# Another pace for the transform steps of the second and the third batch

## The chip, the cores and the metric

One core of one Trainium2 chip runs the kernel. The metric is device time in microseconds (us). TensorE is called PE here, VectorE DVE, ScalarE ACT, GpSimd POOL and SyncE SP; PE and PEld are the products and the weight loads of TensorE.

## The reference

Eight batches of 3136 tokens with 256 channels go through a filter in the frequency domain, and then through a mixing layer and a two-layer perceptron with a residual:

```python
    X = np.fft.rfft(x, axis=1)
    F = (filt_r + 1j * filt_i)[None, :, :]
    Y = X * F
    y = np.fft.irfft(Y, n=x.shape[1], axis=1)
...
    X = np.fft.fft(x, axis=1)
    X = np.fft.fft(X, axis=2)
    mixed = np.real(X).astype(np.float32)
    u = x + mixed
    mu = np.mean(u, axis=-1, keepdims=True)
    var = np.mean((u - mu) ** 2, axis=-1, keepdims=True)
    un = (u - mu) / np.sqrt(var + 1e-06)
    ch = np.maximum(un @ w_ch1, 0.0) @ w_ch2
    return (u + ch).astype(np.float32)
```

The second part's x is the first part's y; `w_ch1` is 256 x 1024, `w_ch2` 1024 x 256.

## The kernel before

All products run in float16 on numbers split into a high and a low part; a product of two split numbers is three matmuls. 3136 is 112 x 28, so each transform is done in two stages of matrix products with a store to DRAM and a load between them.

The work of a batch b has two halves, written as generators whose `yield`s cut them into steps.

*Forth*, `there(b)`, 63 steps (`STEPS`): `forward1` loads the batch in seven parts `x_b_0..6` (L410), takes the greatest absolute value of each on DVE (`absmax`, L289) for a scale, and forms 14 products of the first stage, `s1` (L431), between a split of x into float16 (L425 on ACT, L426 on DVE) and a split of the result (`ast`, L433 and L434) that is stored to `d1` (L435). `forward2` loads it turned (`at`, L456), forms the second stage in seven chunks (`s2`, L481 and L482), multiplies by the filter on DVE and POOL (`yt`, `t`, L491 to L505), folds even and odd parts into a ring of frequencies (`eo`), turns the product with DMA transposes (`z`), and forms the first stage of the inverse (`i1`, L551 to L553), which is stored to `d2` as `bt` (L560).

*Home*, `back(b)`, 17 steps (`BACK`): `inverse2` loads `b2` (L594), forms the second stage of the inverse, `y_b_c` (L617), and stores the scaled result `ys` (L626) to `dy` (L600).

The perceptron takes the 8 x 3136 tokens in 49 groups of 512 (256 slots of two tokens). For a group g: `fetch(g)` loads the filtered tokens y (L687). `prepare(g)` forms the transform over channels, `mix_g` (L700), adds it to y on DVE (L710), normalises (statistics at L769 and L770, scale `sb` at L781 to L785, `un` on ACT at L792), splits the result into `u16` (L795 on ACT, L797 on POOL, on DVE in groups 0 and 1), and turns it by two DMA transposes into `ut` (L804). Then come eight first products `h_g_f` (L828, six matmuls of 512 columns each), each followed by a relu on ACT (L837) and the low part on DVE (L838), and eight second products into `acc_g` (L857, twelve matmuls of 256 columns each), which follow two first products behind (`LAG`). A last add (L866) and a store (L869) end the group.

The order of the work is set in the main loop (L1038 to L1055), which counts first products with q, eight to a group: one first product, a piece of the preparation of the group after next, one second product, one home step if it is due, and then as many forth steps as `advance` is told by a pace (L1051). `bring` (L983) asks for what a fetch needs if the pace hasn't yet brought it. `advance(n)` issues forth steps until n have been issued in all; step n belongs to batch n // 63. It stops ahead of a batch until the home steps of the batch before the last are out, and ahead of a fold while the ring still holds frequencies that a mix needs. Beyond this, a scheduler that works with estimated times settles the order of the instructions on each engine, and semaphores and buffers what waits for what: four PSUM banks are shared in turn by `s1`, `s2`, `i1`, `y` and `mix`, two hold `h`, two `acc`; seven large buffers are shared by x, `at` and `z`. SP issues all loads, stores and transposes in one queue.

Of the kernel before, what the change touches and what calls it, by code (L numbers as in the profile page):

```python
# [38 lines left out]
STEPS = FIRST + PAUSE + 7 * 5  # L39
WAIT = 2  # L40
BACK = 1 + WAIT + 14
EARLY = 0.6
RISE = 28
SOON = 994
LOADED = 300
LOAD_AT = (31, 31, 35, 35, 50, 50, 54, 54)
LOAD_AFTER = (("at", 2), ("at", 2), ("at", 3), ("at", 3), ("bt", 3), ("bt", 3), ("bt", 4), ("bt", 4))
# [142 lines left out]
def program(tc, a, NB):  # L190
    nc = tc.nc
    with ExitStack() as ctx:
        _program(ctx, tc, nc, a, NB)


def _program(ctx, tc, nc, a, NB):
# [482 lines left out]
    def fetch(g):  # L679
        y = ys_of[g] = mp.tile([128, 2, 2, 256], F32, tag="y", name=f"y_{g}", bufs=4)  # L680
        for t, (g0, g1) in enumerate(groups[g]):
            q = g0
            while q < g1:
                b = q // NS
                e = min(g1, (b + 1) * NS)
                with after(("un", 0)) if g == 2 else after(("out", g - 4)):
                    marks["y", g] = nc.sync.dma_start(  # L687
                        y[q - g0 : e - g0, t], dys[b][:, q - b * NS : e - b * NS].rearrange("k s c -> s k c")
                    ).ins
                q = e  # L690
# [123 lines left out]
    def first_product(g, f):  # L814
        y, ut = ready[g]
        m = groups[g][0][1] - groups[g][0][0]
        nt = 2 * sum(g1 - g0 for g0, g1 in groups[g])
        utv = ut[:, : len(groups[g])].rearrange("p t (k d l) q -> p t k d l q", k=2, d=2)
        p = ps_h.tile([128, 512], F32, tag="psh", name=f"h_{g}_{f}")
        even = nt == 2 * m * len(groups[g])  # L820
        runs = [(slice(0, len(groups[g])), 0, nt, m)] if even else [
            (slice(t, t + 1), 256 * t, 2 * (g1 - g0), g1 - g0) for t, (g0, g1) in enumerate(groups[g])
        ]
        for ts, c0, n, m in runs:
            i = 0
            for d in range(2):
                for hw, hx in ((0, 0), (0, 1), (1, 0)):
                    marks["pe"] = nc.tensor.matmul(  # L828
                        p[:, c0 : c0 + n].rearrange("p (t k q) -> p t k q", k=2, q=m),
                        w1s[:, d, hw, 128 * f : 128 * f + 128],  # L830
                        utv[:, ts, :, d, hx, :m],
                        start=i == 0,
                        stop=i == 5,
                    ).ins
                    i += 1
        h = mp.tile([128, 2, 512], F16, tag="h", name=f"h16_{g}_{f}", bufs=4)
        nc.scalar.activation(h[:, 0, :nt], p[:, :nt], AF.Relu)  # L837
        marks["h"] = nc.vector.scalar_tensor_tensor(  # L838
            h[:, 1, :nt], p[:, :nt], 0.0, h[:, 0, :nt], op0=ALU.max, op1=ALU.subtract
        ).ins  # L840
        hs[g, f] = h

    def second_product(g, f):
        tiles = groups[g]
        y = ready[g][0]
        h = hs.pop((g, f))
        if f == 0:
            accs[g] = [
                ps_o.tile([128, 2, 256], F32, tag="pso", name=f"acc_{g}_{t}") for t in range(len(tiles))
            ]  # L850
        c0 = 0
        for t, (g0, g1) in enumerate(tiles):
            m = g1 - g0
            acc = accs[g][t]
            for k in range(2):
                for i, (hh, hw) in enumerate(((0, 0), (0, 1), (1, 0))):
                    nc.tensor.matmul(  # L857
                        acc[:m, k],
                        h[:, hh, c0 : c0 + m],
                        w2s[:, f, hw],  # L860
                        start=f == 0 and k == 0 and i == 0,
                        stop=f == 7 and k == 1 and i == 2,
                    )
                c0 += m
            if f == 7:
                nc.vector.scalar_tensor_tensor(  # L866
                    y[:m, t], acc[:m], beta[:m], y[:m, t], op0=ALU.mult, op1=ALU.add
                )
                marks["sp"] = marks["out", g] = nc.sync.dma_start(a["out"][:, g0:g1].rearrange("k s c -> s k c"), y[:m, t]).ins  # L869
# [86 lines left out]
    def advance(n):  # L956

        while done[0] < min(n, NB * STEPS):
            b, s = divmod(done[0], STEPS)
            if s == 0 and come[0] < BACK * (b - 1) + 1:  # L960
                return
            if s in folds and b * NS + folds[s] - RING > mixed[0]:
                return
            next(forth)
            done[0] += 1

    def give(n):

        while come[0] < min(n, NB * BACK) and done[0] >= STEPS * (come[0] // BACK + 1) - 1:
            next(home)  # L970
            come[0] += 1
# [3 lines left out]
    def need(slot):  # L975

        return BACK * (slot // NS) + 1 + WAIT + 2 + 2 * (slot % NS // 224)

    def soon(slot):

        return max(need(slot), BACK * ((slot + LOADED) // NS) + 1 + WAIT)

    def bring(slot):  # L983
        advance(STEPS * (slot // NS + 1) - 1)
        give(need(slot))
        assert come[0] >= need(slot)
# [48 lines left out]
    for _ in range(AHEAD):  # L1035
        next(work, None)
    per = NS // 32
    for q in range(8 * ng + LAG):  # L1038
        g, f = divmod(q, 8)
        if g < ng:  # L1040
            first_product(g, f)
        if f == 8 - AHEAD:
            for _ in work:
                pass
            if g + 2 < ng:
                work = prepare(g + 2)
        next(work, None)
        if q >= LAG:
            second_product(*divmod(q - LAG, 8))
        give(min(come[0] + 1, soon(32 * q + SOON)))  # L1050
        advance(int(STEPS * (1 + min((q + 1) / RISE, (q + 1) / per + EARLY))))  # L1051
        for ahead in [2] * (q == 0) + [g + 3] * (f == 6):
            if ahead < ng:
                bring(groups[ahead][-1][1] - 1)
                fetch(ahead)  # L1055
# [59 lines left out]
```

## Time and profile before

| | |
|---|---|
| median of 3 runs | 1497.44 us (1496.48 to 1500.48) |
| the profiled execution's own time | 1497.62 us |
| its span, first to last instruction | 1495.8 us |
| PE busy | 1426.8 us, 95% of the span |
| DVE busy | 1101.7 us, 74% |
| ACT busy | 768.5 us, 51% |
| POOL busy | 532.1 us, 36% |
| mean granted clock of PE | 0.984 of full speed |

Busy time is the time in which an engine executes at least one instruction. The granted clock is the share of its full clock that PE was allowed. The page also cuts the span into 40 slices, of 37.4 us each; a digit is the busy share of a slice in tenths:

```profile
PE   8897999959999999999999999999999999999998
DVE  6888878588778786787668787798778886555552
POOL 3840077008600583008600384107710474010110
PEclk9997999989999999999999999999999999999999
```

The ninth digit of PE is the slice from 299 to 337 us. POOL's digits rise and fall with the second stages of the batches, which come in its work as blocks: slices 6 and 7 hold those of the second batch, 10 and 11 those of the third.

### The profile page before, as it was taken

How to read it: one execution, taken by the hardware profiler on the slowest of the kernel's cores; microseconds unless marked ns; L12 is line 12 of the kernel's file. 1: busy time of each engine (PE TensorE's matmuls, PEld its weight loads, DVE VectorE, ACT ScalarE, POOL GpSimd, SP SyncE). 2: the span in 40 equal slices, each digit the busy share in tenths (PEclk: the TensorE clock that was granted, in tenths of full speed). 3: DMA queues.
4: the chain of work that ended last, by engine and by line, in shares of the span. 5: the costliest groups of instructions: out<-in, count | busy, mean ns of one | idle time of the engine just before them, and what ended most of it. 6: DMA issues, size and time to landing. Idle time of an engine off the chain costs nothing.

```text
span 1495.8 us, 30721 instructions
## 1 busy us (share of the span) xinstructions
PE 1426.8 (95%) x11553; PEld 944.6 (63%) x11553; DVE 1101.7 (74%) x2398; ACT 768.5 (51%) x1418; POOL 532.1 (36%) x674
## 2 busy tenths in 40 slices
PE   8897999959999999999999999999999999999998
PEld 3644576536766667666766677667666667666666
DVE  6888878588778786787668787798778886555552
ACT  4764745365536555465545555465545655344331
POOL 3840077008600583008600384107710474010110
PEclk9997999989999999999999999999999999999999
DMA  8866597769884996769874896859775995554320
GB/s 323 282 189 200 144 199 182 228 180 240 191 248 133 213 235 169 219 171 222 193 227 122 215 246 150 255 156 243 181 212 162 226 242 138 161 124 107 87 57 29
DMA packets 445076, 280.46 MB, mean 187 GB/s; under 512 B 218688, under 2 KB 410496, under 8 KB 444928
## 3 DMA queue, kind: packets, MB, share of 16 engines
q1 hardware_dynamic: 444928, 278.51, 71.3%
q8 instruction: 90, 1.47, 0.4%
q14 instruction: 58, 0.48, 0.1%
HBM read 124.78 MB, written 102.79 MB: 152 GB/s over the span
## 4 chain that ended last, share of the span: by engine, by line
PE 64%; DMA 12%; DVE 11%; issue 4%; SPq 3%; ACT 2%; POOL 2%; DVEq 0%; ACTq 0%; POOLq 0%
PE h L828 25%; PE acc L857 24%; DMA x<-x 3%; DMA at<-d 3%; PE y L617 3%; PE s L431 3%; DVE y L710 2%; PE mix L700 2%; DMA d<-ast 2%; DMA z<-y 1%; PE i L551 1%; DVE h L838 1%; DVE mx L289 1%; PE s L481 1%; PE i L553 1%
## 5 line engine op out<-in xcount | busy, mean ns | idle before, releaser
L857 PE MATMUL acc<-w2s,h 128*128 128x256 f16 x4704 | 595.5, 273 | 2.3 <-DVE y L866 1.2
L828 PE MATMUL h<-ut,w1s 128*128 128x512 f16 x2352 | 582.3, 380 | 7.7 <-DVE h L838 6.7
L857 PEld LDWEIGHTS <-h 128*128 128x128 f16 x4704 | 454.5, 98 | 142.0 <-issue 9.0
L837 ACT ACTIVATE h<-h 128x512 f16<-128x512 f32 x392 | 232.8, 595 | 378.6 <-PE h L828 371.1
L838 DVE SCALAR_TENSOR_TENSOR h<-h,h 128x512 f16<-128x512 f32 x392 | 266.7, 682 | 196.1 <-ACT h L837 195.1
L797 POOL TENSOR_TENSOR u<-un,u 128x512 f16<-128x512 f32 x94 | 107.5, 1158 | 767.1 <-ACT u L795 679.4
L828 PEld LDWEIGHTS <-w1s 128*128 128x128 f16 x2352 | 221.3, 98 | 213.4 <-issue 26.2
L710 DVE SCALAR_TENSOR_TENSOR y<-mix,alpha,y 128x508 f32<-128x508 f32 (+1 forms) x368 | 156.1, 474 | 8.4 <-PE mix L700 7.2
L792 ACT ACTIVATE un<-y,sb 128x256 f32<-128x256 f32 x196 | 101.9, 590 | 41.5 <-DVE sb L785 37.1
L505 POOL TENSOR_TENSOR y<-yt,y 128x448 f16<-128x448 f32 x105 | 107.9, 1032 | 21.4 <-ACT y L504 21.2
L626 ACT ACTIVATE ys<-y,alpha 128x512 f32<-128x512 f32 x112 | 76.2, 685 | 72.5 <-PE y L617 71.2
L559 DVE TENSOR_TENSOR bt<-i,bt 112x512 f16<-112x512 f32 x112 | 75.7, 682 | 44.9 <-ACT bt L558 43.3
L499 POOL TENSOR_TENSOR yt<-yt,t 128x224 f32<-128x224 f32 x112 | 76.5, 683 | 72.6 <-DVE t L495 47.5
L491 DVE SCALAR_TENSOR_TENSOR yt<-s,pF,ft 128x448 f32<-128x448 f32 x112 | 75.4, 675 | 29.4 <-PE s L482 23.3
L431 PE MATMUL s<-x,s 112*112 112x512 f16 x294 | 88.2, 390 | 7.6 <-DVE y L710 2.7
L289 DVE TENSOR_REDUCE mx<-x 112x1 f32<-112x1024 f32 x56 | 67.5, 1212 | 33.3 <-DMA x<-x 33.0
L558 ACT CAST bt<-i 112x512 f16<-112x512 f32 x112 | 64.4, 583 | 51.6 <-PE i L553 47.7
L866 DVE SCALAR_TENSOR_TENSOR y<-acc,beta,y 128x512 f32<-128x512 f32 x98 | 71.2, 742 | 24.5 <-PE acc L857 24.4
L481 PE MATMUL s<-s,at 112*128 112x56 f16 x896 | 62.5, 190 | 22.9 <-DMA at<-d 22.0
L434 DVE TENSOR_TENSOR ast<-s,ast 112x512 f16<-112x512 f32 x98 | 66.8, 682 | 22.3 <-ACT ast L433 21.9
L504 ACT CAST y<-yt 128x448 f16<-128x448 f32 x112 | 62.8, 564 | 39.2 <-POOL yt L500 38.2
L433 ACT CAST ast<-s 112x512 f16<-112x512 f32 x98 | 57.0, 582 | 47.5 <-PE s L431 40.6
(137 smaller groups left out, 1729.7 us busy)
## 6 DMA issues: line engine op xcount, KB each, us to landing
x<-x SPq DMA_DIRECT2D x56, 512.0 KB
at<-d SPq DMA_DIRECT2D x56, 512.0 KB
b<-d SPq DMA_DIRECT2D x56, 512.0 KB
d<-ast SPq DMA_DIRECT2D x112, 224.0 KB
d<-bt SPq DMA_DIRECT2D x112, 224.0 KB
out<-y SPq DMA_DIRECT2D x98, 256.0 KB
y<-dy SPq DMA_DIRECT2D x92, 256.0 KB
dy<-ys SPq DMA_DIRECT2D x208, 112.0 KB
```

The lines of the kernel that those rows point to most:

```text
L289: nc.vector.tensor_reduce(dst, src, axis=axis, op=ALU.max, apply_absolute_value=True)
L431: nc.tensor.matmul(p, s1[:, hs], x16[:, hx], start=i == 0, stop=i == 2)
L481: nc.tensor.matmul(o, w, s2[:, U, 0].rearrange("p (r k) -> p r k", r=2), start=True, stop=False)
L499: nc.gpsimd.tensor_tensor(yh[:, 0], yh[:, 0], t2v[:, 1], op=ALU.subtract)
L505: last = half(b, hf == 1).tensor_tensor(ylo, ytv, yhi, op=ALU.subtract)
L710: nc.vector.scalar_tensor_tensor(out, p, al, y, op0=ALU.mult, op1=ALU.add)
L792: nc.scalar.activation(un[:m, k], y[:m, t, k], AF.Identity, bias=sb[:m, i, 1:2], scale=sb[:m, i, 3:4])
L797: marks["u16", g] = low.tensor_tensor(u16[:m, :, :, 1], unv, u16[:m, :, :, 0], op=ALU.subtract).ins
L828: marks["pe"] = nc.tensor.matmul(p[:, c0 : c0 + n].rearrange("p (t k q) -> p t k q", k=2, q=m), w1s[:, d, hw, 128 * f : 128 * f + 128], ut ...
L837: nc.scalar.activation(h[:, 0, :nt], p[:, :nt], AF.Relu)
L838: marks["h"] = nc.vector.scalar_tensor_tensor(h[:, 1, :nt], p[:, :nt], 0.0, h[:, 0, :nt], op0=ALU.max, op1=ALU.subtract).ins
L857: nc.tensor.matmul(acc[:m, k], h[:, hh, c0 : c0 + m], w2s[:, f, hw], start=f == 0 and k == 0 and i == 0, stop=f == 7 and k == 1 and i == 2,)
```

## The change

The pace of the forth steps is a new function of the count of first products, with three lines of which the lowest holds.

```diff
+HEAD = 8
+HOLD = 36
+CATCH = 32
...
     per = NS // 32
+
+    def pace(q):
+
+        second = STEPS + HEAD + (STEPS - HEAD) * q / RISE
+        third = 2 * STEPS + max(0, q - HOLD) * STEPS / CATCH
+        return min(second, third, STEPS * (1 + EARLY + q / per))
+
     for q in range(8 * ng + LAG):
...
-        advance(int(STEPS * (1 + min((q + 1) / RISE, (q + 1) / per + EARLY))))
+        advance(int(pace(q + 1)))
```

With `STEPS` 63, `RISE` 28, `EARLY` 0.6 and `per` 49: before, 65 steps were out after the first product 0 (two of the second batch), 63/28 = 2.25 more after each product, and all 126 of two batches at product 28; the third batch went on at that pace until the other line, 63/49 = 1.29 steps a product, came below it at product 39. Now 72 are out after product 0 (nine of the second batch), 55/28 = 1.96 more after each, and 126 at product 28 as before; then none until product 36, and from there 63/32 = 1.97 a product until the line of 1.29 is met at product 67. At product 39 the third batch is 19 steps behind where it was. From there on, the fourth batch and all later ones go as before. Line numbers of the changed kernel are higher by 3, from the loop on by 10.

On the engines the order differs from the first group's products to about group 16. Three places of it:

On DVE, in the first group's hidden tiles (`h16_0_f`, the low part of hidden tile f of group 0; `mx_1<-x_1_q`, absmax of part q of the second batch; `y_1`, adds of group 1). Before:

```order
L838 SCALAR_TENSOR_TENSOR h16_0_0_1682<-h_0_0_1675,h16_0_0_1682 128x512
L770 BN_AGGR mv_1_1651<-st_1_1652 128x2
L769 BN_STATS st_1_1652<-y_1_1622 128x6 x2
L838 SCALAR_TENSOR_TENSOR h16_0_1_1712<-h_0_1_1705,h16_0_1_1712 128x512
L289 TENSOR_REDUCE mx_1_1699<-x_1_0_1692 112x1
L770 BN_AGGR mv_1_1651<-st_1_1652 128x2 x2
L838 SCALAR_TENSOR_TENSOR h16_0_2_1725<-h_0_2_1718,h16_0_2_1725 128x512
L289 TENSOR_REDUCE mx_1_1699<-x_1_1_1693 112x1
L289 TENSOR_REDUCE mx_1_1699<-x_1_2_1694 112x1
```

and now:

```order
L841 SCALAR_TENSOR_TENSOR h16_0_0_1682<-h_0_0_1675,h16_0_0_1682 128x512
L292 TENSOR_REDUCE mx_1_1699<-x_1_0_1692 112x1
L292 TENSOR_REDUCE mx_1_1699<-x_1_1_1693 112x1
L292 TENSOR_REDUCE mx_1_1699<-x_1_2_1694 112x1
L292 TENSOR_REDUCE mx_1_1699<-x_1_3_1695 112x1
L292 TENSOR_REDUCE mx_1_1699<-x_1_4_1696 112x1
L713 SCALAR_TENSOR_TENSOR y_1_1622<-mix_1_1625,alpha_0_373,y_1_1622 128x2x127 x2
L713 SCALAR_TENSOR_TENSOR y_1_1622<-mix_1_1625,alpha_0_373,y_1_1622 128x4
L292 TENSOR_REDUCE mx_1_1699<-x_1_5_1697 112x1
L773 BN_AGGR mv_1_1651<-st_1_1652 128x2 x2
L841 SCALAR_TENSOR_TENSOR h16_0_1_1723<-h_0_1_1716,h16_0_1_1723 128x512
```

Five reductions moved ahead of the second hidden tile and of the last adds of group 1; before, the first of them stood behind that tile, in ones and twos.

On SP, behind the last stores of the second batch's first inverse stage (`b2_1_c`, loads of its home transform; `x_2_q`, loads of the third batch; `ut_5`, transposes of group 5). Before:

```order
L594 DMA b2_1_0_3330<-d2_1_130 128x8x256
L410 DMA x_2_0_3332<-x 128x1024
L410 DMA x_2_1_3333<-x 128x1024
L410 DMA x_2_2_3334<-x 128x1024
L410 DMA x_2_3_3335<-x 128x1024
L410 DMA x_2_4_3336<-x 128x1024
L410 DMA x_2_5_3337<-x 128x1024
L594 DMA b2_1_1_3411<-d2_1_130 128x8x256
L804 DMA_TRANSPOSE ut_5_3352<-u16_5_0_3453 128x8x128
L804 DMA_TRANSPOSE ut_5_3352<-u16_5_1_3495 128x8x128
```

and now the place at which the loads of the third batch stand, behind the fetches of group 6 and among those of group 7:

```order
L597 DMA b2_1_3_3526<-d2_1_130 128x8x256
L690 DMA y_7_3735<-dy_1_3329 128x2x256
L603 DMA dy_1_3329<-ys_1_4_3528 28x4x256 x4
L413 DMA x_2_0_3658<-x 128x1024
L413 DMA x_2_1_3659<-x 128x1024
L413 DMA x_2_2_3660<-x 128x1024
L413 DMA x_2_3_3661<-x 128x1024
L413 DMA x_2_4_3662<-x 128x1024
L690 DMA y_7_3735<-dy_1_3329 128x2x256
L597 DMA b2_1_4_3767<-d2_1_130 128x8x256
L413 DMA x_2_5_3663<-x 128x1024
```

The loads of x moved from ahead of the transposes of group 5 to behind them, by some twenty rows.

On DVE, the preparation of group 6 (`y_6`, its adds; `st_6`, `mv_6`, its statistics; `ast_2`, `x16_2`, splits of the third batch's first stage; `h16_g_f`, low parts). Before:

```order
L838 SCALAR_TENSOR_TENSOR h16_5_7_4374<-h_5_7_4367,h16_5_7_4374 128x512
L434 TENSOR_TENSOR ast_2_2_3598<-s1_2_2_3594,ast_2_2_3598 112x2x256
L426 SCALAR_TENSOR_TENSOR x16_2_5_3706<-x_2_2_3334,sx_2_3530,x16_2_5_3706 112x512
L710 SCALAR_TENSOR_TENSOR y_6_3436<-mix_6_3612,al_6_0_3751,y_6_3436 128x4x127
L710 SCALAR_TENSOR_TENSOR y_6_3436<-mix_6_3612,al_6_0_3751,y_6_3436 128x2x127 x2
L710 SCALAR_TENSOR_TENSOR y_6_3436<-mix_6_3612,al_6_0_3751,y_6_3436 128x4
L710 SCALAR_TENSOR_TENSOR y_6_3436<-mix_6_3612,alpha_1_2225,y_6_3436 128x4x127
L866 SCALAR_TENSOR_TENSOR y_5_3002<-acc_5_0_4043,beta_96,y_5_3002 128x512
L866 SCALAR_TENSOR_TENSOR y_5_3002<-acc_5_1_4044,beta_96,y_5_3002 128x512
L710 SCALAR_TENSOR_TENSOR y_6_3436<-nyq_6_0_3621,alpha_1_2225,keep_6_3749 1x2x127
L769 BN_STATS st_6_3814<-y_6_3436 128x6
L710 SCALAR_TENSOR_TENSOR y_6_3436<-mix_6_3612,alpha_1_2225,y_6_3436 128x2x127 x2
```

and now its end:

```order
L841 SCALAR_TENSOR_TENSOR h16_4_7_3745<-h_4_7_3738,h16_4_7_3745 128x512
L772 BN_STATS st_6_3679<-y_6_3419 128x6 x2
L292 TENSOR_REDUCE mx_2_3665<-x_2_0_3658 112x1
L772 BN_STATS st_6_3679<-y_6_3419 128x6
L292 TENSOR_REDUCE mx_2_3665<-x_2_1_3659 112x1
L773 BN_AGGR mv_6_3678<-st_6_3679 128x2 x2
L292 TENSOR_REDUCE mx_2_3665<-x_2_2_3660 112x1
L841 SCALAR_TENSOR_TENSOR h16_5_0_3787<-h_5_0_3780,h16_5_0_3787 128x512
L773 BN_AGGR mv_6_3678<-st_6_3679 128x2
L292 TENSOR_REDUCE mx_2_3665<-x_2_3_3661 112x1
L292 TENSOR_REDUCE mx_2_3665<-x_2_4_3662 112x1
L841 SCALAR_TENSOR_TENSOR h16_5_1_3828<-h_5_1_3821,h16_5_1_3828 128x512
```

The adds of group 6 moved from behind group 5's last hidden tile, among the first-stage steps of the third batch, to ahead of group 4's last hidden tile, where no such step stands; the reductions of the third batch now stand around group 5's first. On PE, the mix of group 6 goes with them, from product 47 to product 37, the first y product of the second batch from product 37 to 34, and the mix of group 7 stands directly ahead of the first product of group 6.

## The prediction

> **What bounds the kernel now.** I read the head of the page first, then the idle time of the PE stage by stage, then the waits behind it.
>
> The page, its head and one group row:
>
> ```profile
> span 1495.8 us, 30721 instructions
> PE 1426.8 (95%) x11553; PEld 944.6 (63%) x11553; DVE 1101.7 (74%) x2398; ACT 768.5 (51%) x1418; POOL 532.1 (36%) x674
> ...
> L289 DVE TENSOR_REDUCE mx<-x 112x1 f32<-112x1024 f32 x56 | 67.5, 1212 | 33.3 <-DMA x<-x 33.0
> ```
>
> PE is busy for 95% of the span, so a new order of the same work can win only what PE loses: 1495.8 - 1426.8 = 69.0 us of idle time, and what a reduced clock adds to its busy time. The windows show where that lies in the stretch that the change touches. The columns are start and end, length, then busy time and instructions of PE, PEld, DVE, ACT and POOL, the granted clock of PE, DMA share and GB/s:
>
> ```profile
> 130.00:150.00 20.00, 20.00 (x133) 12.60 (x132) 20.00 (x44) 5.72 (x10) 0.00 (x0) 1.00 0.26 69
> 150.00:160.00 10.00, 6.33 (x33) 3.50 (x31) 8.35 (x32) 8.49 (x17) 0.00 (x0) 0.84 0.61 157
> ...
> 180.00:200.00 20.00, 18.83 (x187) 12.63 (x185) 16.74 (x41) 8.49 (x16) 4.26 (x6) 1.00 0.74 182
> 200.00:230.00 30.00, 29.60 (x329) 22.41 (x328) 24.24 (x51) 14.39 (x28) 28.67 (x41) 1.00 0.94 195
> 230.00:260.00 30.00, 27.83 (x241) 20.61 (x238) 27.06 (x54) 17.25 (x36) 23.20 (x30) 1.00 0.75 178
> 260.00:290.00 30.00, 27.14 (x190) 17.13 (x188) 15.17 (x23) 9.20 (x17) 2.27 (x2) 1.00 0.93 275
> ...
> 300.00:325.00 25.00, 19.22 (x110) 10.08 (x108) 23.74 (x51) 15.80 (x28) 0.00 (x0) 0.93 0.62 183
> 325.00:340.00 15.00, 4.03 (x78) 3.69 (x77) 8.67 (x29) 7.52 (x15) 2.95 (x4) 0.70 0.81 187
> 340.00:380.00 40.00, 39.73 (x395) 26.68 (x393) 34.51 (x67) 23.05 (x45) 38.27 (x51) 0.99 1.15 245
> ```
>
> Length less PE's busy time is its idle time. The great loss is a **hole from 300 to 340 us**: 5.78 + 10.97 = 16.75 us idle in two rows, a quarter of all of it, and PE's work in it ran at a clock of 0.93 and 0.70. Afterwards (340 to 380) 0.27 us is lost. Inside the hole, PE's timeline (start, duration, line, tiles, count, and in brackets the wait before it):
>
> ```profile
> 303.40 0.56 PE L700 MATMUL mix<-mix,eo 128*128 128x129 f16 x8
> ...
> 307.19 1.46 PE L431 MATMUL s<-x,s 112*112 112x512 f16 x6
> 311.35 1.07 PE L431 MATMUL s<-x,s 112*112 112x512 f16 x4 [2.69 <-DVE y L710]
> ...
> 325.17 0.95 PE L700 MATMUL mix<-mix,eo 128*128 128x129 f16 x16
> 336.92 0.23 PE L481 MATMUL s<-s,at 112*128 112x56 f16 x1 [10.79 <-DMA at<-d]
> ```
>
> and SyncE's queue, which issues the loads and the transposes:
>
> ```profile
> 263.19 3.18 SPq L410 DMA_DIRECT2D x<-x  x6
> 266.41 1.25 SPq L594 DMA_DIRECT2D b<-d  x1
> 267.76 9.48 SPq L804 DMA_TRANSPOSE ut<-u  x2
> ...
> 332.26 1.02 SPq L456 DMA_DIRECT2D at<-d  x2
> 333.32 3.50 SPq L804 DMA_TRANSPOSE ut<-u  x1
> ```
>
> At 303.40 PE forms the mix of group 6; that group's second transpose is issued at 333.32 and takes 3.50, so its first product can't start before 336.8, 33.4 us later. No first product is left for PE in that time: group 5's are over. It has only the third batch's first stage (L431), whose steps go through the same DVE as the adds of group 6, and then waits for the loads of the second stage (L481, the 10.79). DVE is busy 23.74 of 25 us. So two chains end there, group 6's preparation and the third batch's forward transform, each slowed by the other, and PE has run out of both. The preparation was late since its mix stands only one product ahead of its first product, behind the second batch's last steps.
>
> **The change part by part.** No instruction is added or removed; all terms below are PE idle time or clock. The sum is made against the profiled execution's own 1497.62 us (1.8 us more than its span); the median of the runs, 1497.44, is the same within 0.2.
>
> *The hole.* The second batch now ends its steps 9 steps ahead at the start and at 1.96 a product in place of 2.25, both reaching its end at product 28; but its last chunk, its home transform and the mix of group 6 come earlier in the order (mix 6 at product 37, before at 47), since steps of the third batch no longer stand between. Group 6's preparation so gets eleven products of cover, not one. Two rows price a product:
>
> ```profile
> 217.08 1.30 PE h L828 x6
> 218.38 1.31 PE acc L857 x12
> ```
>
> These six first and twelve second products take 2.61 us, eight of each 20.9. Eleven products are 28.7 us before any transform work; with the y products and the third batch's first stage among them they exceed 33.4. Group 6 therefore doesn't wait. The next in line is group 7: its mix now stands directly ahead of group 6's first product, its preparation runs beside the s1 steps (33 products of 0.217, 7.2 us, lie there), as group 6's did. Cover: 20.9 + 7.2 + some 3 of mix and y products = 31; need: 33.4 by group 6's measure, less where the absmax and part of the s1 steps are out of the way, 31. I take 1.0 us of wait, ends 0 and 4. The wait of the second stage for its loads stays in some size, as in other batches:
>
> ```profile
> 194.91 0.20 PE L481 MATMUL s<-s,at 112*128 112x56 f16 x1 [0.37 <-DMA at<-d]
> ...
> 502.00 0.20 PE L481 MATMUL s<-s,at 112*128 112x56 f16 x1 [1.90 <-DMA at<-d]
> ```
>
> I take 1.9 (ends 0.4 and 4). So 16.75 becomes 2.9: **-13.9**.
>
> *Clock in the hole.* 19.22 x 0.07 + 4.03 x 0.30 + 39.73 x 0.01 = 2.95 us of busy time were lost to it. That goes with the waits: -3.0.
>
> *The y products of the second batch.* The first of them needs the last inverse chunk through a store and a load:
>
> ```profile
> 257.52 0.11 PE i L553
> ...
> 259.44 0.92 SPq L560 DMA_DIRECT2D d<-bt  x2
> 262.69 0.38 SPq L594 DMA_DIRECT2D b<-d  x1
> ...
> 266.95 1.06 PE L617 MATMUL y<-b,i 112*64 112x256 f16 x12 [0.51 <-DMA b<-d]
> ```
>
> From 257.6 to 266.95 are 9.3 us, which before are covered but for 0.51. In the new order PE has about 5.6 us of other work between the two (two products of 2.61 and a rest). Its queue stands still behind this wait, first products included. 0.51 becomes 3.7: **+3.2**, ends 0 and 5. A wait of this size costs clock as well: the 2.69 above and the small ones around it went with 0.93, 19.22 x 0.07 = 1.35 us. I add +1.4. [...]
>
> *Start.* The second batch's absmax reductions (1.21 us each by the L289 row) are issued earlier: five stand between the DVE parts of the first and second hidden tile of group 0, where before there was none. Rows of before:
>
> ```profile
> 139.74 3.46 DVE L289 TENSOR_REDUCE mx<-x 112x1 f32<-112x1024 f32 x3
> ...
> 153.50 0.38 PE L285 MATMUL pb_x<-row_x,ones 1*128 1x2 f32 x2 [1.36 <-DVE row_x L278]
> 155.59 0.38 PE L431 MATMUL s<-x,s 112*112 112x512 f16 x1 [1.71 <-ACT x L425]
> ```
>
> Before, PE is idle 3.67 us in 150 to 160, none in 130 to 150. Now the five take 5 x 1.15 (three in 3.46) = 5.8 us, in which PE has two hidden tiles in buffers and then stands, about 5 us; the scale is ready sooner, so that the waits at 153 to 156 go. 3.67 becomes 5.0: +1.3, ends -3.7 and +5.
>
> *The second batch's spectrum.* In 230 to 260 DVE is 27.06 of 30 busy and PE idle 2.17. At 1.96 steps a product DVE has room: half goes, -1.0 (ends -2 and +1). POOL, gap-free at 28.67 of 30 in 200 to 230, gets fewer steps a product too.
>
> *SyncE's queue.* Six x loads stood ahead of group 5's transposes (9.48 us from issue of the first to the end of the second); now they stand behind them, and the loads of x come between y fetches of group 7. PE lost 0.40 there (below), and DVE waits for x as before: 0, ends -1 and +2.
>
> *Boundaries.* Before groups 8, 9 and 12 no second product of the group ahead is left to fill a late transpose; before it was so ahead of 5. There it cost:
>
> ```profile
> 275.34 1.48 PE L857 MATMUL acc<-w2s,h 128*128 128x256 f16 x12 [0.78 <-DVE h L838]
> ...
> 279.50 2.75 PE L828 MATMUL h<-ut,w1s 128*128 128x512 f16 x12 [0.40 <-DMA ut<-u]
> ```
>
> Some 0.4 each, +1.0 in all (ends 0 and 3.5). From group 16 on both orders agree.
>
> **Sum:** -13.9 - 3.0 + 3.2 + 1.4 + 1.3 - 1.0 + 0 + 1.0 = -11.0, 1486.6 us.
>
> **The rivals.** *Half comes back.* Groups 7 and 8 are both late by 4 us, since the third batch's steps, now at 1.97 a product where they were at 1.29 from product 39 on, keep DVE full through both. For it: DVE 23.74 of 25 in the hole. Against: 340 to 380 ran with POOL at 38.27 and DVE at 34.51 of 40 and PE lost 0.27. It adds 3 us at group 7 (4 for 1.0) and 3 at group 8: 1492.6, chance 0.18.
>
> *No change.* The preparation is bound by DVE wherever it stands: the hole moves to product 56 with 11 us of idle time and its clock. 1497.6, chance 0.09. Against it stand the eight products of cover that group 6 lacked.
>
> *Slower.* Group 7's preparation takes place beside all of s1 and stretches beyond 33.4 us, and PE, with the third batch's second stage behind h 7 in its queue, stands for both as it does now: the 16.75 and the 3.0 stay, the 5 of the start and 3.2 + 1.4 of the y products come on top. About 1507. It decides from the point where preparation 7 takes over 31 + 14 = 45 us. Chance 0.11.
>
> *That the change does nothing* is excluded by the order: the steps do move.
>
> **How the numbers follow.** Forecast 0.62, rivals 0.18, 0.09, 0.11. The forecast's own ends: with the low ends of the start (5.0 less than taken) and of the y products with their clock (4.6 less) 1477; with the high ends of group 7 and the start (3.0 and 3.7 more) 1493.3. To leave out no more than 2 in 10 the range takes in the second rival and the third: 1475 to 1498. What this kernel's runs can tell from no change is about 0.3%, 4.5 us. Faster by more than that (below 1493): 0.60 of the forecast and 0.14 of the first rival, 0.74; within: 0.14; slower: 0.12.
>
> **What would show it.** Right: no wait over 4 us of PE between group 5's and group 8's first products, clock 1.00 there; the first y product of the second batch waiting some 3.7 us for its load; the first s2 product of the third batch waiting about 2. Wrong: a long wait of the first product of group 7 for its transpose, with DVE over 95% busy ahead of it; PE idle over 6 us between 130 and 160; or a second stage that waits for loads 10 us again.

## The result and the profile after

| | before | changed |
|---|---|---|
| median of 12 runs each | 1498.12 us | 1508.03 us (1503.72 to 1517.76) |
| ratio | | 1.0071, 95% interval 1.0055 to 1.0086 |
| span of the profiled execution | 1495.8 us | 1505.1 us |
| PE busy | 1426.8 us | 1426.5 us |
| PE idle in the span | 69.0 us | 78.6 us |

The change makes the kernel about 10 us slower. PE does the same work in nearly the same busy time; its idle time grew by 9.6 us. The forecast was 11 us the other way, and the time lies outside its range.

The hole is gone. These are the windows of the changed kernel that answer to those shown of before:

```profile
130.00:150.00 20.00, 13.94 (x72) 7.71 (x70) 17.06 (x39) 6.17 (x13) 0.00 (x0) 0.83 0.17 48
150.00:160.00 10.00, 10.00 (x78) 6.95 (x76) 7.68 (x16) 6.91 (x12) 0.00 (x0) 1.00 0.36 75
...
230.00:260.00 30.00, 23.63 (x243) 19.27 (x242) 27.06 (x62) 15.10 (x29) 28.28 (x38) 0.93 0.82 180
260.00:290.00 30.00, 28.11 (x198) 16.73 (x198) 13.90 (x35) 14.28 (x26) 2.27 (x2) 0.96 0.74 207
...
300.00:325.00 25.00, 25.00 (x170) 16.67 (x169) 16.17 (x37) 13.58 (x24) 2.27 (x2) 0.93 0.45 130
325.00:340.00 15.00, 15.00 (x96) 9.18 (x96) 14.96 (x35) 9.05 (x18) 0.00 (x0) 1.00 0.48 145
...
345.00:460.00 115.00, 100.46 (x907) 69.28 (x906) 84.49 (x176) 52.02 (x99) 60.68 (x79) 0.97 0.89 218
460.00:580.00 120.00, 114.98 (x999) 77.08 (x997) 97.26 (x213) 66.33 (x125) 55.81 (x73) 0.99 0.76 186
```

and the two last stretches in the kernel before:

```profile
345.00:460.00 115.00, 114.59 (x946) 78.45 (x945) 88.75 (x187) 58.91 (x112) 57.33 (x75) 1.00 0.88 215
460.00:580.00 120.00, 117.00 (x1038) 79.78 (x1037) 95.44 (x204) 67.90 (x129) 60.91 (x79) 1.00 0.80 191
```

From 300 to 340 us PE lost 16.75 us before and loses nothing now. But from 345 to 460 it lost 0.41 and now loses 14.54, behind that 5.02 in place of 3.00, and from 230 to 260 it loses 6.37 in place of 2.17. The clock, 0.93 and 0.70 in the two rows of the hole, is now below 1 in six of the eight rows. PE's timeline has the waits (the second number from the left is the duration, the bracket the wait):

```profile
140.97 1.44 PE L831 MATMUL h<-ut,w1s 128*128 128x512 f16 x3 [5.63 <-DVE h L841]
...
258.70 0.43 PE L554 MATMUL i<-z,i 112*112 112x256 f16 x1 [5.87 <-DMA z<-y]
...
353.62 4.36 PE L831 MATMUL h<-ut,w1s 128*128 128x512 f16 x12 [2.00 <-DMA ut<-u]
...
383.17 0.32 PE L554 MATMUL i<-z,i 112*112 112x256 f16 x1 [1.64 <-DMA z<-y]
...
409.45 0.43 PE L554 MATMUL i<-z,i 112*112 112x256 f16 x1 [3.00 <-DMA z<-y]
424.04 2.32 PE L831 MATMUL h<-ut,w1s 128*128 128x512 f16 x10 [1.49 <-DMA ut<-u]
...
437.96 1.06 PE L620 MATMUL y<-b,i 112*64 112x256 f16 x12 [1.60 <-DMA b<-d]
...
454.31 1.46 PE L831 MATMUL h<-ut,w1s 128*128 128x512 f16 x6 [2.11 <-DVE h L841]
459.57 1.03 PE L860 MATMUL acc<-w2s,h 128*128 128x256 f16 x8 [1.63 <-DVE y L869]
```

In place of the one wait of 10.79 us there are now a dozen of 0.5 to 3 us between 345 and 580 us, with five releasers. The first product of group 6 starts at 319.6 us, 20.6 earlier than before (340.2). That of group 7 is 13.8 earlier, of group 8 10.8, of group 9 2.2 later, of group 16 11.2 later. About 10.5 us of this turn is PE work that stood ahead of group 6 before and stands behind it now (33 matmuls of s1, the first 64 of s2 and 15 of the second products); the rest is the new waits and their clock.

### The profile page after: what moved, and what is told of

It reads as the page before. It is cut to its first block, busy times and chain, and to the rows that moved or that the text cites. A ratio compares the mean times of both kernels' runs of the same rounds, so it can differ in the third digit from the quotient of the medians.

```text
span 1505.1 us, 30700 instructions
## 1 busy us (share of the span) xinstructions
PE 1426.5 (95%) x11553; PEld 944.7 (63%) x11553; DVE 1100.4 (73%) x2398; ACT 767.3 (51%) x1418; POOL 533.1 (35%) x674
## 4 chain that ended last, share of the span: by engine, by line
PE 63%; DMA 12%; DVE 10%; POOL 5%; issue 4%; ACT 3%; SPq 2%; DVEq 0%; ACTq 0%; POOLq 0%
PE h L831 24%; PE acc L860 24%; PE s L434 3%; PE y L620 3%; DMA x<-x 2%; DMA at<-d 2%; DVE y L713 2%; PE mix L703 2%; DVE mx L292 1%; DMA d<-ast 1%; DMA z<-y 1%; DMA out<-y 1%; DVE h L841 1%; POOL ef L526 1%; PE i L554 1%
## 5 line engine op out<-in xcount | busy, mean ns | idle before, releaser
L831 PE MATMUL h<-ut,w1s 128*128 128x512 f16 x2352 | 588.2, 383 | 25.1 <-DVE h L841 16.8
L629 ACT ACTIVATE ys<-y,alpha 128x512 f32<-128x512 f32 x112 | 75.9, 685 | 67.2 <-PE y L620 64.8
L554 PE MATMUL i<-z,i 112*112 112x256 f16 x224 | 62.3, 278 | 16.7 <-DMA z<-y 12.9
L620 PE MATMUL y<-b,i 112*64 112x512 f16 (+1 forms) x480 | 70.5, 382 | 6.6 <-DMA b<-d 6.6
```

Source lines behind the costliest of these rows:

```text
L554: nc.tensor.matmul(p[:, i], i1[:, j + i, 0], z[:, i, 0], start=True, stop=False)
L620: marks["i2"] = nc.tensor.matmul(p[64 * h : 64 * h + 64, js], i2[:, t, h, i], bt[:, o + js.start : o + js.stop, h], start=i == 0, stop=i == 1,
L831: marks["pe"] = nc.tensor.matmul(p[:, c0 : c0 + n].rearrange("p (t k q) -> p t k q", k=2, q=m), w1s[:, d, hw, 128 * f : 128 * f + 128], ut ...
```

## The experiments

All kernels ran beside the kernel before on the same chip; a ratio of 0.001 is 1.5 us. The three columns of idle time are PE's, in the stretch of the hole (230 to 345 us) and in two behind it, each from one profile, length less busy time. "Steps" is the third batch's pace per first product.

| kernel | ratio to before (95%) | 230 to 345 | 345 to 460 | 460 to 580 | steps |
|---|---|---|---|---|---|
| before | 1 | 21.97 | 0.41 | 3.00 | 2.25, 1.29 from 39 |
| changed | 1.0071 (1.0055 to 1.0086) | 11.13 | 14.54 | 5.02 | 1.97 from 36 |
| e1, second batch's part only | 0.9994 (0.9974 to 1.0013) | 16.36 | 2.19 | 3.67 | 2.25, 1.29 from 39 |
| e2, third batch's part only | 1.0023 (1.0000 to 1.0045) | 9.80 | 15.14 | 3.99 | 1.97 from 36 |
| e3, second as before | 0.9985 (0.9962 to 1.0007) | 9.30 | 14.40 | 1.27 | 1.58 from 32 |
| e4, second as before | 0.9971 (0.9951 to 0.9990) | 10.68 | 5.78 | 7.36 | 1.43 from 36 |
| e5, changed, mixes earlier | 1.0052 (1.0028 to 1.0076) | 10.32 | 14.67 | 5.13 | 1.97 from 36 |
| e6, changed, start spread | 1.0021 (1.0003 to 1.0040) | 9.10 | 16.44 | 4.05 | 1.97 from 36 |
| e7, changed, u16 on DVE | 1.0073 (1.0043 to 1.0102) | 9.82 | 13.83 | 5.88 | 1.97 from 36 |
| e8, e5 and e6 together | 1.0084 (1.0065 to 1.0103) | 9.41 | 14.08 | 7.47 | 1.97 from 36 |
| e9, changed, slower catch-up | 0.9995 (0.9978 to 1.0012) | 9.72 | 2.49 | 7.93 | 1.43 from 36 |
| e10, e9 with the start spread | 0.9973 (0.9953 to 0.9992) | 9.03 | 3.29 | 7.11 | 1.43 from 36 |
| e11, second as before | 1.0046 (1.0022 to 1.0069) | 9.97 | 18.09 | 2.83 | 2.63 from 36 |
| e12, second as before | 1.0058 (1.0035 to 1.0081) | 9.35 | 6.44 | 2.56 | 1.31 from 32 |

### The two parts apart

The first edit leaves the new line of the second batch alone, the second that of the third:

```diff
 # e1
-        third = 2 * STEPS + max(0, q - HOLD) * STEPS / CATCH
-        return min(second, third, STEPS * (1 + EARLY + q / per))
+        third = STEPS * (1 + q / RISE)
+        return min(second if q < RISE else third, STEPS * (1 + EARLY + q / per))
 # e2
-        second = STEPS + HEAD + (STEPS - HEAD) * q / RISE
+        second = STEPS * (1 + q / RISE)
```

> The second batch's new pace alone; the third batch starts at product 28 with 2.25 steps a product as before. Theory A (each part costs on its own: the head costs the 5.63 at the start and the 5.87 at the second batch's last z, the hold fills the hole but its steeper pace brings waits from 340 to 580 us): the hole of about 11 us ahead of group 6 is back, the two early waits are as in the changed kernel, no waits of ut between groups 7 and 13: about 1504 us. Theory B (the head costs nothing in the end, all is the hold's): 1498. Theory C (the head alone does the harm): 1508 or more.

> The third batch's hold and pace alone; the second batch as before. Theory A: no wait of 5 us at the start, none of the second batch's last z, no hole ahead of group 6, but 16 us of waits between 340 and 580 us as in the changed kernel: about 1499. Theory B: 1508. Theory C: 1486.

Measured: 1498.23 and 1501.64 us against 1498.04. Neither part alone makes the loss, so C falls, and B with its 1508 for the third part. A was near for e2, wrong for e1: there the hole didn't come back in full. From 300 to 345 us PE is idle 16.75 us before, 4.95 in e1 and 4.76 in e2. **Each part fills some 12 us of the same hole**; both together can win no more than its 16.75, but pay both prices. That is 7 us less won than the sum of the two, and the ratios say the same: -0.0006 and +0.0023 add up to +0.0017, the two together give +0.0071, 8 us more (the three intervals together leave 5 us either way). The prices can be read from the two stretches. First e1:

```profile
230.00:345.00 115.00, 98.64 (x744) 63.60 (x743) 86.26 (x189) 59.06 (x109) 35.09 (x44) 0.88 0.75 201
345.00:460.00 115.00, 112.81 (x968) 77.64 (x966) 91.35 (x193) 59.49 (x113) 62.17 (x81) 1.00 0.92 219
```

then e2:

```profile
230.00:345.00 115.00, 105.20 (x772) 68.85 (x771) 86.88 (x179) 59.77 (x110) 29.39 (x35) 0.99 0.72 193
345.00:460.00 115.00, 99.86 (x877) 68.62 (x877) 80.09 (x175) 51.76 (x99) 58.44 (x77) 0.96 0.87 213
```

The second batch's part costs ahead of 345 us (its waits of 5.63 at the start and 5.76 for the last z are those of the changed kernel, and the clock goes to 0.88, though in the changed kernel to 0.94 only); the third batch's part costs behind it, 15.14 us in place of 0.41.

### The pace of the third batch

```diff
 # e3, e4, e11, e12: e2 with other constants
-HOLD = 36
-CATCH = 32
+HOLD, CATCH = 32, 40   # e3
+HOLD, CATCH = 36, 44   # e4
+HOLD, CATCH = 36, 24   # e11
+HOLD, CATCH = 32, 48   # e12
 # e9: the changed kernel with this alone
-CATCH = 32
+CATCH = 44
```

> The second batch as before; the third held to product 32 and then 1.575 steps a product in place of 1.97 from 36. Theory A (the waits from 340 to 580 us come from the steep pace, which puts the spectrum of the third batch, bound by POOL, into the banks ahead of the mixes of groups 8 and 9): the hole stays away or is under 6 us, the waits of 340 to 580 fall below 8: about 1490. Rival D (the waits come from the hold itself, whatever the pace behind it): 1498 as the hold alone.

> The second batch as before; the third held to product 36 and then 1.43 steps a product. Theory A: no wait of ut before groups 7 to 12, those of 340 to 580 below 6 us, 1486; a later wait for the third batch's y products may cost 3. Rival D: 1500 or more, as the third batch's home transform comes later still.

> The changed kernel with 1.43 steps a product from product 36 in place of 1.97, the head kept. Theory P (the idle time from 345 to 460 us is set by the third batch's steps per first product, apart from the head): it falls from 14.5 to under 6 us, all else as in the changed kernel; the hold alone won 7.8 us by this, so about 1500. Rival K (idle time of PE between 230 and 460 us is conserved, about 24 us in whatever order, as the moved mixes suggest): 1506 to 1508.

> The second batch as before, the third held to 36 and then faster: 2.63 steps a product, which meets the old line at product 52 in place of 67. Theory P: idle time from 345 to 460 us at least the 16 of the hold alone, 1502 or more. Rival L (lateness: the third batch being behind its old line costs, not the pace): under 10 us, 1496.

With the hold at product 36, idle time from 345 to 460 follows the pace: 18.09 us at 2.63 steps a product, 15.14 (14.54 with the head) at 1.97, 5.78 (2.49 with the head) at 1.43. The next stretch takes a part of that back: from 460 to 580 us it is 7.36 (7.93 with the head) at 1.43 and 2.83 to 5.02 at the steeper paces. Over both stretches the gentle pace so saves 6.0 us (9.1 with the head) against 1.97. The rows of e11 (first) and e9:

```profile
345.00:460.00 115.00, 96.91 (x850) 66.55 (x851) 80.69 (x175) 48.93 (x94) 59.60 (x79) 0.90 0.88 214
```

```profile
345.00:460.00 115.00, 112.51 (x1025) 78.87 (x1024) 83.38 (x189) 58.41 (x110) 60.73 (x79) 1.00 0.86 208
```

POOL's busy time is the same, 59.60 and 60.73 us: the same spectrum of the third batch lies in both. PE's instructions aren't: 850 against 1025. The traces show why. From the first s2 product of the third batch to its last i1 product 73.2 us pass in e11, 69.5 in the changed kernel, 70.6 in e9, 77.2 in e4 and 74.0 before; in these five the stage takes 70 to 77 us whatever pace is asked for. What the pace sets is how many first products stand in the same stretch of PE's order: 14, 16, 19, 21 and 20. With 14 PE has 61.4 us of work in it and is idle 11.7, with 16 62.9 and 6.6, with 19 to 21 69.4 to 74.0 and 0.4 to 3.2. A steep catch-up takes the cover away from a stage that it didn't make shorter here. All fourteen kernels fit the count: 14 to 17 products go with 13.83 to 18.09 us idle from 345 to 460, 18 to 21 with 0.41 to 6.44. That the pace makes the loss is shown; that it does so by this count is argued, as no run changes the count alone.

K (conserved idle time) falls by e9: 11.4 us below the changed kernel by the ratios, all of it from this number alone. L falls by e11, which is back at its old line at product 52 and idles most in this stretch (18.09 us, 1503.41 us in all). e4 is 0.29% below the kernel before, a third of the way that A had put it (1486). e3 missed: 1497.90 us against 1490, with one wait of 7.53 us for the ut of group 7. At its 1.58 steps a product, from 32 on, the second stage runs 64.8 us with 16 products and only 3.3 us idle; 7.5 of the stretch's 14.40 us stand ahead of it, as group 7's preparation falls among the first stage's steps. So the pace of the catch-up isn't all. 1498 was also the number of D (the hold itself), which falls by e4 alone: 1493.84 us where it gave 1500 or more.

> The second batch as before, the third held to 32 only and then 1.31 steps a product, the pace that all later batches have. Theory P: idle time from 345 to 460 us under 6, the hole filled: 1491 to 1494, the best of all. Rival K: 1498.

e12 missed as well, on the other side: 1502.97 us. In the stretch it does nearly what was expected (6.44 us idle, under 6 expected), and the first product of group 16 starts at 596.1 us, 20.6 earlier than before. It is all lost later. One row of e12 and the same of before:

```profile
620.00:1300.00 680.00, 652.22 (x5410) 441.29 (x5408) 516.31 (x1131) 358.34 (x668) 261.48 (x331) 0.99 0.78 194
```

```profile
620.00:1300.00 680.00, 669.33 (x5589) 450.42 (x5588) 520.48 (x1142) 370.70 (x685) 263.74 (x333) 1.00 0.77 196
```

27.8 us idle against 10.7. The line of e12 at 1.31 steps a product never meets the old one (1.29) within the kernel, so that all batches stay behind it, by some 16 steps at first. That this lateness is what costs the 17 us wasn't tried apart. e4, e9 and e10 meet the old line at about product 180.

### Where the waits within a pace come from

The prediction had priced the drained boundaries ahead of groups 8 and 9 at 0.4 us each. The mixes of groups 4 and 9 start at 225.7 and 388.7 us in the changed kernel, 11.1 and 12.6 later than before, each 2.0 and 2.2 us after the last read of the bank that it takes over from a spectrum chunk (223.7 and 386.6). Before, mix 4 took over a bank of the inverse stage, and mix 9 one that had been free for 3.9 us. POOL's timeline shows what follows for group 4, its low parts of u in the changed kernel

```profile
251.71 1.16 POOL L800 TENSOR_TENSOR u<-un,u 128x512 f16<-128x512 f32 x1 [0.56 <-ACT u L798]
252.83 1.03 POOL L508 TENSOR_TENSOR y<-yt,y 128x448 f16<-128x448 f32 x1
253.82 1.15 POOL L800 TENSOR_TENSOR u<-un,u 128x512 f16<-128x512 f32 x1
```

and before:

```profile
241.83 1.16 POOL L797 TENSOR_TENSOR u<-un,u 128x512 f16<-128x512 f32 x1 [3.19 <-ACT u L795]
...
243.94 1.16 POOL L797 TENSOR_TENSOR u<-un,u 128x512 f16<-128x512 f32 x1
```

Ten us late, group 4's first product no longer stands ahead of the last i1 chunk of the second batch in PE's order, and PE waits 5.87 us for that chunk's z with nothing else to do. Three kernels tried this:

```diff
 # e5
-        if f == 8 - AHEAD:
+        if f == (0 if g in (2, 6, 7) else 8 - AHEAD):
 # e6
+        second = min(second, STEPS + 1 + 3 * q)
         return min(second, third, STEPS * (1 + EARLY + q / per))
 # e7
-            low = nc.vector if g < 2 else nc.gpsimd
+            low = nc.vector if g < 14 else nc.gpsimd
```

> The changed kernel with the mixes of groups 4, 8 and 9 issued two products earlier in the program, so that fewer spectrum steps stand ahead of them in the rotation of the four banks. Theory M (a mix waits for the bank of a spectrum chunk that POOL hasn't let go, its group's preparation is late, PE has no second product left and stands in the spectrum's own waits): the 5.87 us wait for the second batch's last z falls under 1.5, the idle time of PE from 340 to 460 us (14.5) falls below 8: about 1497 against 1508. Rival Q (POOL's queue delays the u16 of these groups, wherever their mix stands): less than 3 us won, 1505 or more.

> The changed kernel with the low part of u on DVE in place of POOL in groups 2 to 13. Rival Q: the waits for ut before groups 7 to 13 and the 5.87 go, 1496. Theory M: a part of the waits for ut goes, since the low part no longer stands behind the spectrum on POOL, but the mixes are as late as before and DVE has 12 us more to do: 1503 to 1510.

e5 did with the three places what M said: no wait for the last z of the second batch, none for ut before groups 8 and 9. It won little, 1505.91 us (ratio 1.0052). Its waits behind the hole, on PE:

```profile
357.19 0.20 PE L484 MATMUL s<-s,at 112*128 112x56 f16 x1 [2.80 <-DMA at<-d]
...
411.31 0.29 PE L554 MATMUL i<-z,i 112*112 112x256 f16 x1 [3.35 <-DMA z<-y]
...
455.49 2.72 PE L831 MATMUL h<-ut,w1s 128*128 128x512 f16 x6 [4.50 <-DVE h L841]
```

Other tiles wait, and their sum is the same: 14.67 us against 14.54; ahead of 345 us the 5.87 came back as waits of the third batch's first stage, 10.32 against 11.13. So M holds for the place of a wait and falls as its price. Q falls with e7, which takes the low part off POOL (53.0 us busy from 345 to 460 in place of 60.7) and is no faster, 1509.29 us. All of these, with e6 and e8 below, have 14 to 17 products beside the third batch's second stage, and the idle time from 345 to 460 us stays at 13.8 to 16.4 us while its releasers change. It needn't lie in the stage: in e7 7.52 us of it are one wait for the ut of group 7 ahead of the stage, which then runs 61.5 us with 2.7 idle. Why the sum stays is open.

### The start

> The changed kernel with the second batch's first steps spread at three a product in place of nine at once; its line is met after some seven products. If the five reductions at once are what PE waits for in group 0, the 5.63 goes and the two waits ahead of group 1 come back in part (3.67 before): 2 to 5 us won, about 1504. Rival: DVE's work ahead of group 1 is the bound whatever its order: the wait moves, 1508. Theory M expects nothing from it in 230 to 460 us, except where the spread moves a mix.

> Mixes of groups 4, 8 and 9 earlier and the start spread, both on the changed kernel. If the two costs are apart, their gains add up: 1508 - 11 - 4 = 1493, faster than the kernel before. If the gain of the hole was already spent, no faster than 1498.

> The changed kernel with both: 1.43 steps a product from product 36, and the second batch's first steps spread at three a product. If the two add up, 7 us below the former: about 1493. If the spread's gain was only a shift of later waits, about 1500.

e6 is 7.5 us below the changed kernel by the ratios (1.0021 against 1.0071). The 5.63 is gone, three waits of about 1 us in group 0 stand in its place; from 130 to 160 us idle time is the same, and the clock is not. First e6, then the changed kernel:

```profile
130.00:160.00 30.00, 24.07 (x155) 14.97 (x154) 27.96 (x70) 13.71 (x26) 0.00 (x0) 1.00 0.24 58
```

```profile
130.00:160.00 30.00, 23.94 (x147) 14.66 (x146) 24.73 (x54) 13.08 (x24) 0.00 (x0) 0.89 0.23 57
```

0.11 of 23.94 is 2.6 us. Group 4's first product starts at 256.7 in place of 261.3, and the wait for the last z is 2.44 in place of 5.87, as mix 4 stands earlier too. How the gain divides between the two wasn't taken apart. e8, with the moved mixes on top, loses all of it again: 1509.48 us, where 1493 was expected if gains added up. Its profile is 6.2 us longer than that of e6. Ahead of 120 us, where both have done the same 746 matmuls, e8 is busy 2.9 us more and idle 2.9 us less (100.63 and 97.69 busy, at 0.94 and 0.96); no edit reaches there. Behind 120 us it has 3.6 us more idle time and 2.6 us more busy time. Why its waits fall so stays open. On the slower catch-up the spread adds less than on the changed kernel: e10 has 1492.32 us, ratio 0.9973, 2.2 parts in a thousand or 3.3 us below e9. The 1493 that was expected for it came about because e9 was already faster than its own 1500. With e4 it is the best, faster than both kernels; the interval of each reaches the other's ratio, so that they aren't told apart.

## Why the prediction was wrong

- *The hole, -13.9.* Right in kind and more: the two windows lose nothing, and the first product of group 6 is 20.6 us earlier. The s2 wait of 1.9 and group 7's wait of 1.0 came as 0 and 2.00. Ahead of the hole, from 290 to 300 us, two waits for DVE's low parts came that the prediction didn't have: 2.87 us idle in place of 0.19.
- *What stands next.* This step failed. The prediction stopped at group 7, with +1.0 for all "boundaries" (0.4 each, from the one drained boundary of before). Measured from 345 to 580 us: 14.54 + 5.02 - 0.41 - 3.00 = +16.2 us, and e9, which changes that pace alone, is 11.4 us faster. A row of the kernel before that had PE 39.73 of 40 busy, 340 to 380, was taken as a sign that a dense spectrum costs nothing. There the third batch's second stage had 20 first products beside it; the new pace leaves it 16. The rival that gave half of the hole back named the steeper pace and put it on DVE at groups 7 and 8, for 6 us; DVE is busy 84.49 of 115 us there, less than before (88.75). The slower rival, the hole moving whole to group 7, did not happen: that group waits 2.00 us (7.53 in e3 and 7.52 in e7). That its 1507 lies near the measured 1508.03 is luck.
- *The second batch's spectrum, -1.0.* Wrong in sign. It was argued from the room on DVE; but the nine steps of head put more spectrum ahead of mix 4, and 230 to 260 lost 6.37 in place of 2.17: +4.2.
- *The y products, +3.2 and their clock.* Wait of 0.38, not 3.7: the 5.87 us at the i1 chunk just ahead, which the prediction didn't see, let no more of it show.
- *Start, +1.3.* The five reductions took the about 5 us that were foreseen (5.63) and the later waits went: 6.06 in place of 3.67, +2.4. The clock was not counted: 0.11 of 23.94 us, where before lost 0.05 of 26.33.
- *Clock, -3.0 + 1.4.* Wrong in sign. The hole's loss went, but the clock is 0.93, 0.96, 0.93 and 0.97 in four rows of the changed kernel (230 to 290, 300 to 325, 345 to 460). The busy time of the whole profile hides this, since ahead of 120 us, where both kernels have done the same 746 matmuls, the profile of before ran at the lower clock (1.4 us more), and again behind group 16 (1.6 us). The rows up to 120 us and from there to the first product of group 16, where both have done the same work, with length, PE's busy time and matmuls (one record apart), clock, DMA share and GB/s; before, then changed:

```profile
0.00:120.00 120.00, 101.52 (x746) 0.93 0.82 268
120.00:616.66 496.66, 461.10 (x3807) 0.97 0.79 200
0.00:120.00 120.00, 100.16 (x746) 0.97 0.81 267
120.00:627.84 507.84, 463.81 (x3808) 0.96 0.76 195
```

Behind 120 us and up to group 16 busy time grew by 2.7 us, where -1.6 was forecast, and idle time by 8.5. The clock fell behind waits of 2 to 3 us too, as it had around the long one of 10.79 us (0.70 from 325 to 340 us before). In the changed kernel, around the waits of 2.00 us (ended at 353.62) and of 3.00 us (409.45):

```profile
351.20:354.60 3.40, 1.41 (x9) 1.00 0.79 217
354.60:358.00 3.40, 3.40 (x11) 0.50 0.69 203
405.80:409.20 3.40, 0.65 (x26) 1.00 1.09 256
409.20:412.60 3.40, 3.15 (x11) 0.50 0.99 119
```

Each of these two drops to 0.50 stands behind a single wait, the first behind one of 2.00 us.

## What to carry to other kernels

A long wait on the bound engine shows that the work beside a slower chain is too little there; moving the chain moves the shortage. Count what stands beside the chain in its new place (here first products beside the second transform stage) before taking the wait as won. Two edits that fill the same hole don't add up, but their prices do, so each is to be run alone; and a held-back stage should resume at a pace at which its cover lasts (1.43 steps a product was the best here), not at one that catches up fast.

## What was not expected of the hardware

PE's idle time stayed within 3 us while mixes were moved, the u split changed its engine and the start was spread (14.54, 14.67, 13.83 and 14.08 us from 345 to 460, 16.44 in e6), with the waits on different tiles each time.

What a wait cost in clock went with how it fell. In the profiles of before and of the changed kernel the clock is 1.00 or 0.50 and changes on a grid of 3.41 us (whole stretches at 0.50 took 3.41, 6.83, 10.24, 13.65 and 17.07 us). From 130 us on, a step of that grid at full clock with 2.0 us or more of PE idle time was followed by a step at half clock in 7 of 7 cases of the two profiles, one with less than 1.5 us in none of 769, and in between in 3 of 8. In the changed kernel the wait of 2.00 us at 353.62 lies in one step and cost a step at half clock; the one of 2.11 us at 454.31 is cut by the grid into 1.37 and 0.74 and cost none. How much of this is chance shows ahead of 110 us, where ten of the fourteen profiles have done the same 739 matmuls: the clock there is 0.95 to 0.98, and PE's busy time 96.05 (e12) to 99.42 us (e2).
